# Strassen's form of the last FFN's output product, and a filter product in quarters of the array

## The chip, the core and the metric

The kernel runs on one core of a Trainium2 chip. The metric is the device time of one execution in microseconds, as the median of several executions. The engines are called PE (TensorE; PEld is its weight load), DVE (VectorE), ACT (ScalarE), POOL (GpSimd) and SP (SyncE); SP, ACT and POOL also issue DMAs.

## What is computed

The reference has two blocks, in fp32. The first is a long convolution with a filter that a small MLP makes; the second is a maxout FFN over all tokens of its result.

```python
# x, v: (4, 12544, 128); pos_emb: (12544, 64); w1: (64, 64); w2: (64, 128)
h_filt = (np.maximum(pos_emb @ w1, 0.0) @ w2) * np.exp(-0.01 * pos)[:, None]
u = x * v
y = irfft(rfft(u, n=2 * S, axis=1) * rfft(h_filt, n=2 * S, axis=0), n=2 * S, axis=1)[:, :S]
z = (x * y).reshape(4 * 12544, 128)
# moe_w1, moe_w2, moe_w3: (128, 768); moe_w_out: (768, 128)
out = np.maximum(np.maximum(z @ moe_w1, z @ moe_w2), z @ moe_w3) @ moe_w_out
```

## The kernel before

**The Fourier transform** has length 128 x 90 and is done in two steps by matrix products: a first one with `f1`/`f1h` (`first_halves`, L141), twiddle products with a table `wt` in 45 pieces `g` (`g_second`, `g_third`, both through `halves_mm`, L132), and a last one with `f4`/`f4p` (`t_last`). `halves_mm` puts a 128-column weight as two matmuls of 64 columns into the two column halves of the array. Each fp32 matmul shows as two instructions (two passes) in the trace.

**The order of work** is written out by hand; each engine runs its instructions in that order.
- *Start.* 30 warm-up products on zeros, then eight pairs of `mlp_in` (PE, L303: quarters on the diagonal, posT as the weight) and `mlp_out` (DVE, L311: relu and window). `window_back`, two small PE steps that turn the window around, stands behind the first `mlp_in`. Then the first transform of the filter's hidden units and of batch 0's `u`, with the conversion of the FFN weights on DVE beside it.
- *Filter and batch 0.* A loop over `s` of 45 pieces and three to drain. In each, PE runs `g_third(0, s-3)`, `s_second(s)` (L674: the filter's second transform step, real and imaginary parts in the two column halves), `g_second(s)` and `s_filter(s-1)` (L688: the product with w2, here `w2x`, which holds w2 twice, once with a minus sign on the real half, so that both parities of the spectrum come out of one product with K = 128 and 256 columns). ACT copies out `zs` (L444, then it issues its DMA), `G` (L678), `eo` (L163), makes `xs` (L413, L414) and copies `ht` (L693). DVE runs the butterfly (L157, L158), then `g_re` (L419), `g_im` (L423, L424) and `g_unfold` (L431); POOL issues the two DMAs of `ht` to `hd` (L695).
- *FFN.* 128 tiles of 392 tokens (32 per batch). The maximum of three is taken as one part plus the maximum of 0 and two differences: `w_sb[1]` and `w_sb[2]` hold differences to `w_sb[0]`, and `lin` = w1 times w_out is the linear part. For each of six blocks `f` of 128 hidden units, `up` runs two products (pa, pb), ACT takes relu of pa (L545), DVE the maximum with pb (L548); one step later `down` adds the product with `wo_sb[:, f]` to `ops`. Behind the last block ACT copies `ot` (L561) and issues its DMA. `t_load` (SP) fetches a tile's `zt` and `xT`; `t_last` makes its input `g` two steps ahead of use. Beside the FFN of batches 0 to 2 the next batch's convolution runs (`conv_steps`); beside that of batch 3, nothing. There POOL is idle.

Of the kernel before, what the change touches and what calls it, by code (L numbers as in the profile page):

```python
# [9 lines left out]
FP32 = mybir.dt.float32  # L10
# [5 lines left out]
P = 128  # L16
# [54 lines left out]
def kernel(  # L71
# [42 lines left out]

    w_sb = [const.tile([D, DFF], FP32, name=f"w_sb{i}") for i in range(3)]
    wo_sb = const.tile([P, NF, D], FP32, name="wo_sb")
    lin = const.tile([D, D], FP32, name="lin")
    eye = const.tile([P, P], FP32, name="eye")
    f1 = const.tile([NB, 2 * N1], FP32, name="f1")
# [105 lines left out]
    pro = ExitStack()  # L225
    pin = pro.enter_context(tc.tile_pool(name="pin", bufs=1))
    lwp = pro.enter_context(tc.tile_pool(name="lwp", bufs=3))
    fin = ExitStack()
# [13 lines left out]
    w2_in = sml.tile([P, D], FP32, name="w2_in")  # L242
    w2x = pin.tile([P, 2, D], FP32, name="w2x")
    win = sml.tile([64 + HH, P], FP32, name="win")
# [44 lines left out]

    def signs():  # L290

        for sg, lo_, m in ((0, 0, 1.0), (0, FO, 1.0), (1, 0, -1.0), (1, FO, 1.0)):
            nc.scalar.mul(w2x[lo_:lo_ + FO, sg].rearrange("f (c g) -> f c g", c=GC),
                          w2_in[lo_:lo_ + FO].rearrange("f (g c) -> f c g", c=GC), m)


# [216 lines left out]
    def t_last(i):  # L513
        zt = zts.pop(i)
        ps = cps.tile([P, 512], FP32, tag="cv", name="yps")
        g = hp.tile([D, 4, NB], FP32, tag="g", name="gt", bufs=2)
        y = ps[:, 0:N].rearrange("d (p n) -> d p n", p=4)
# [21 lines left out]

    def up(i, f):  # L540
        rhs = gs[i][:].rearrange("d p n -> d (p n)")
        h = hp.tile([P, N], FP32, tag="hid", name="hid")
        pa = hps.tile([P, 512], FP32, tag="hps", name="pa")
        halves_mm(pa[:, 0:N], w_sb[1][:, f * P:(f + 1) * P], rhs, True, True)
        nc.scalar.activation(h[:], pa[:, 0:N], Relu)  # L545
        pb = hps.tile([P, 512], FP32, tag="hps", name="pb")
        halves_mm(pb[:, 0:N], w_sb[2][:, f * P:(f + 1) * P], rhs, True, True)
        nc.vector.tensor_tensor(out=h[:], in0=h[:], in1=pb[:, 0:N], op=ALU.max)  # L548
        return h

    def down(i, f, h):
        if f == 0:
            pos_[i] = ops.tile([D, 512], FP32, tag="ops", name="ops")
            halves_mm(pos_[i][:, 0:N], lin[:], gs[i][:].rearrange("d p n -> d (p n)"), True,
                      False)
        halves_mm(pos_[i][:, 0:N], wo_sb[:, f, :], h[:], False, f == NF - 1)
        if f < NF - 1:
            return
        gs.pop(i)
        o = op_.tile([D, 4, NB], FP32, tag="o", name="ot")  # L560
        nc.scalar.copy(o[:].rearrange("d p n -> d (p n)"), pos_.pop(i)[:, 0:N])  # L561
        dst = outT.rearrange("d (p b n) -> d p b n", b=B, n=NB)[:, 4 * i[1]:4 * i[1] + 4, i[0], :]
        nc.scalar.dma_start(dst, o[:])

    def run(steps):
# [34 lines left out]

    warm_up(30)
    raws.append(load_raw(*jobs[0], nc.sync))
# [5 lines left out]
    for i in range(9):  # L608
        if i < 8:
            mlp_in(i)  # L610
        if i == 0:
            window_back()
        if i:
            mlp_out(i - 1)
    signs()
    mps.close()
# [42 lines left out]
    pl = sps.tile([D, 512], FP32, name="pl")  # L659
    Gs = {}  # L660

    def fold(f):
# [4 lines left out]
        return lambda: halves_mm(pl[:, 0:D], w1t[:, 0], wo_sb[:, f, :], f == 0, f == NF - 1)  # L667

    def s_second(g):

        ps = gps.tile([P, 512], FP32, tag="g", name="gps")
        for k in range(2):
            for r in range(2):
                nc.tensor.matmul(ps[64 * r:64 * r + 64, k * P:(k + 1) * P],  # L674
                                 specH[:, 2 * g + k, r, :], wf[g][:, k, r, :],
                                 start=(k == 0), stop=True, skip_group_check=True)
        G = cvp.tile([P, 2, 2, 64], FP32, tag="G", name="G", bufs=2)
# [3 lines left out]
    def s_filter(g):  # L681

        G = Gs.pop(g)
        ps = sps.tile([P, 1024], FP32, tag="h", name="sps")
        for c in range(2):
            for k in range(2):
                for h in range(2):
                    nc.tensor.matmul(  # L688
                        ps[64 * h:64 * h + 64, (2 * c + k) * 2 * D:(2 * c + k + 1) * 2 * D],
                        G[:, k, c], w2x[:].rearrange("p s d -> p (s d)"), start=(k == 0),  # L690
                        stop=True, skip_group_check=True)
        ht = cvp.tile([P, 2, 2, 2, D], FP32, tag="ht", name="ht", bufs=2)
        nc.scalar.copy(ht[:].rearrange("p c k q d -> p (c k q d)"), ps[:])  # L693
        for c in range(2):
# [6 lines left out]
    muls = dict(zip((NK - 13, NK - 11, NK - 10, NK - 5, NK - 3, NK - 1), range(EARLY)))  # L701
    turns = {NK - 9: 0, NK - 4: 2}
    for s in range(NK + 3):
        if s >= 3:
# [4 lines left out]
        if s < NK:  # L709
            ws[s, 0] = wf[s]  # L710
            s_second(s)
            g_second(s)
            wf.pop(s)
# [35 lines left out]

    hp = ctx.enter_context(tc.tile_pool(name="hp", bufs=3))  # L750
    f4p = hp.tile([N1, 2, NB // 2], FP32, name="f4p", bufs=1)
    nc.scalar.dma_start(f4p[:], f4p_d)
    inq = ctx.enter_context(tc.tile_pool(name="inq", bufs=2))
    planes = [hp.tile([P, 2, 4, P], U16, name=f"planes{i}", bufs=1) for i in range(3)]
    for t in planes:
        nc.gpsimd.memset(t[:].rearrange("p h s n -> p (h s n)"), 0)
    op_ = ctx.enter_context(tc.tile_pool(name="op", bufs=2))
    wp = ctx.enter_context(tc.tile_pool(name="wp", bufs=3))
    hh = ctx.enter_context(tc.tile_pool(name="hh", bufs=3))
    cvp = ctx.enter_context(tc.tile_pool(name="cvp", bufs=3))  # L760
    cps = ctx.enter_context(tc.tile_pool(name="cps", bufs=4, space=PSUM))
    hps = ctx.enter_context(tc.tile_pool(name="hps", bufs=3, space=PSUM))
    ops = ctx.enter_context(tc.tile_pool(name="ops", bufs=1, space=PSUM))
    state = {"turn": cps, "pair": (wp, hh), "cv": (cvp, cps), "xb": 3}


    tiles = [(b, i) for b in range(B) for i in range(NT)]
    late = None
    for n, (b, i) in enumerate(tiles):
        if i == 0:  # L770
            beside = {}
            if b + 1 < B:
                beside = conv_steps(b + 1, EARLY if b == 0 else 0)
        if n == 0:
# [3 lines left out]
        for f in range(NF):  # L778
# [9 lines left out]
            late = ((b, i), f, h)  # L788
            if f == 3 and n + 1 < len(tiles):
                t_last(tiles[n + 1])  # L790
            s = i * NF + f
            run(beside.pop(s, ()))
            if s == NT * NF - 1:
                assert not beside, sorted(beside)
    down(*late)


# [35 lines left out]
```

## Time and profile before

| | us |
|---|---|
| median of 4 runs | 2415.91 (2413.43 to 2422.55) |
| the profiled execution | 2414.46 |
| its span in the profile | 2412.3 |
| PE busy | 2394.4 |
| DVE busy | 1286.0 |
| ACT busy | 1026.5 |
| POOL busy | 314.3 |

The span runs from the first to the last instruction of the program; the profiled execution's own time has 2.2 us more around it. In lines of the timeline the columns are the start, the duration, the engine, the source line and the operation with its output and inputs, the number of instructions merged, and in brackets the engine's idle time before it with what ended it. Matmuls are pipelined, so their durations overlap, and the distance of starts is their pace. In a table by stretches the columns are the stretch, its length, busy time and instructions of PE, PEld, DVE, ACT and POOL, the granted TensorE clock, the DMA share and GB/s. Lines of the chain hold start, duration and work.

### The profile page before, as it was taken

Reading aid. Unit: us, or ns where it says so; the run is one execution under the profiler, and the core shown is the slowest. Engines: PE = TensorE matmul, PEld = TensorE weight load, DVE = VectorE, ACT = ScalarE, POOL = GpSimd, SP = SyncE. Lnnn points to the kernel's source line nnn. Section 1 sums busy time; section 2 is a strip of 40 time slices with the busy share of each in tenths; the row PEclk is TensorE's granted clock in tenths of the full one; section 3 lists DMA queues with packets and bytes.
Section 4 is the critical chain, followed back from the end, with each engine's and each line's share of the span. In section 5 each row is a group of like instructions: output and inputs, shape, how many; then the busy total and the mean of one; then the engine's idle time right before and its main releaser. Section 6 shows DMA issues by size and latency. Waiting matters only on the chain.

```text
span 2412.3 us, 63290 instructions
## 1 busy us (share of the span) xinstructions
PE 2394.4 (99%) x26089; PEld 1464.8 (61%) x26089; DVE 1286.0 (53%) x2719; ACT 1026.5 (43%) x1981; POOL 314.3 (13%) x349
## 2 busy tenths in 40 slices
PE   8999999999999999999999999999999999999999
PEld 7988866665555646666656546666665654444444
DVE  4678844456666635446666644546666642222222
ACT  2688843344444434444444424444444432222222
POOL 1022211011111111101111111101111100000000
PEclk9999999999999999999999999999999999999999
DMA  6878979777777659967787859978777842222221
GB/s 147 202 219 268 291 162 185 162 190 195 210 195 214 179 116 191 180 172 212 207 218 203 228 125 179 192 157 219 210 216 211 211 116 62 54 63 53 64 53 36
DMA packets 544553, 408.21 MB, mean 169 GB/s; under 512 B 390244, under 2 KB 436381, under 8 KB 544265
## 3 DMA queue, kind: packets, MB, share of 16 engines
q1 hardware_dynamic: 421760, 315.25, 54.7%
q10 hardware_dynamic: 117129, 74.31, 10.7%
q0 software_dynamic: 5376, 14.62, 2.2%
q8 instruction: 205, 3.36, 0.6%
q14 instruction: 83, 0.68, 0.1%
HBM read 295.76 MB, written 84.67 MB: 158 GB/s over the span
## 4 chain that ended last, share of the span: by engine, by line
PE 97%; DMA 1%; ACT 0%; DVE 0%; issue 0%; ACTq 0%; POOL 0%; SPq 0%; DVEq 0%
PE ops L132 24%; PE pb L132 21%; PE pa L132 21%; PE ps L132 13%; PE ps L141 8%; PE yps L132 5%; PE sps L688 3%; PE pm L303 1%; PE pst L341 1%; PE gps L674 1%; DMA specH<-in_pos_emb_dram 0%; DMA zd<-zs 0%; DMA hd<-ht 0%; DMA ut<-in_xr_dram 0%; ACT ht L693 0%
## 5 line engine op out<-in xcount | busy, mean ns | idle before, releaser
L548 DVE TENSOR_TENSOR hid<-hid,pb 128x392 f32<-128x392 f32 x768 | 431.8, 562 | 789.2 <-PE pb L132 506.1
L545 ACT ACTIVATE hid<-pa 128x392 f32<-128x392 f32 x768 | 381.9, 498 | 797.8 <-PE pa L132 628.4
L132 PE MATMUL pa<-gt,w_sb 128*64 128x392 f32 x3072 | 640.6, 493 | 0.7 <-DVE gt L533 0.7
L132 PE MATMUL pb<-gt,w_sb 128*64 128x392 f32 x3072 | 639.6, 492 | 1.4 <-ACT hid L545 1.2
L132 PE MATMUL ops<-hid,wo_sb 128*64 128x392 f32 x3072 | 639.5, 492 | 0.1
L132 PEld LDWEIGHTS pb<-gt,w_sb 128*64 128x64 f32 x3072 | 225.7, 137 | 283.1 <-issue 256.4
L132 PEld LDWEIGHTS ops<-hid,wo_sb 128*64 128x64 f32 x3072 | 226.8, 137 | 279.2 <-issue 228.4
L424 POOL TENSOR_TENSOR xt<-xt,xs 128x512 f32<-128x512 f32 x135 | 172.3, 1277 | 969.0 <-DVE xs L423 774.0
L132 PEld LDWEIGHTS pa<-gt,w_sb 128*64 128x64 f32 x3072 | 201.7, 137 | 110.9 <-issue 67.5
L141 PEld LDWEIGHTS ps<-f,uT 98*64 98x64 f32 x4096 | 178.1, 137 | 47.5 <-issue 44.8
L132 PEld LDWEIGHTS ps<-ab,wt 128*64 128x64 f32 x2880 | 168.6, 137 | 51.2 <-issue 26.6
L132 PE MATMUL ps<-ab,wt 128*64 128x128 f32 x2880 | 190.8, 274 | 1.0 <-DVE ab L431 0.9
L132 PEld LDWEIGHTS ps<-spec,wt 128*64 128x64 f32 x2880 | 168.0, 137 | 37.9 <-issue 34.2
L132 PE MATMUL ps<-spec,wt 128*64 128x128 f32 x2880 | 189.4, 273 | 1.4 <-issue 1.4
L141 PE MATMUL ps<-f,uT 98*64 98x90 f32 x4096 | 188.3, 241 | 0.0
L449 DVE TENSOR_TENSOR zs<-ps,z 128x256 f32<-128x256 f32 x270 | 102.0, 419 | 96.7 <-ACT z L447 94.5
L413 ACT ACTIVATE xs<-xt 64x512 f32<-64x512 f32 x180 | 113.2, 629 | 72.2 <-DVE xt L158 59.8
L431 DVE TENSOR_TENSOR ab<-xt 128x256 f32<-128x256 f32 x360 | 136.0, 419 | 1.6
L356 POOL COPY planes<-ut 128x784 uint16<-128x784 uint16 x90 | 76.5, 850 | 426.7 <-DVE ut L336 306.9
L419 DVE TENSOR_TENSOR xt<-xt,ht 128x512 f32<-128x512 f32 x180 | 124.2, 690 | 14.3 <-ACT ht L693 13.9
L145 ACT COPY spec<-ps 128x360 f32<-128x360 f32 (+1 forms) x132 | 71.7, 546 | 136.1 <-PE ps L141 136.0
L132 PEld LDWEIGHTS yps<-f4p,zt 90*64 90x64 f32 x3072 | 107.2, 138 | 34.5 <-issue 33.1
(86 smaller groups left out, 1827.7 us busy)
## 6 DMA issues: line engine op xcount, KB each, us to landing
wt<-wt_const SPq DMA_DIRECT2D x360, 256.0 KB, 4.8
ht<-hd SPq DMA_DIRECT2D x270, 256.0 KB, 4.7
zd<-zs ACTq DMA_DIRECT2D x180, 256.0 KB, 4.7
zt<-zd SPq DMA_DIRECT2D x192, 180.0 KB, 4.0
ut<-in_xr_dram SPq DMA_DIRECT2D x128, 196.0 KB, 3.7
ut<-in_vr_dram SPq DMA_DIRECT2D x128, 196.0 KB, 4.3
xT<-in_x_dram SPq DMA_DIRECT2D x512, 49.0 KB, 3.2
out_dram<-ot ACTq DMA_DIRECT2D x128, 196.0 KB, 4.0
```

Of the source, the lines that this page charges most:

```text
L132: nc.tensor.matmul(out[64 * h:64 * h + 64], lhsT[:, 64 * h:64 * h + 64], rhs, start=start, stop=stop, skip_group_check=True)
L141: nc.tensor.matmul(ps[64 * c:64 * c + 64, 256 * i + r * N1:256 * i + (r + 1) * N1], a[:, r, :], table[:, c * N1:(c + 1) * N1], start=(i % ...
L145: copy(dst, ps[:].rearrange("p (s m) -> p s m", m=256)[:, :, 0:2 * N1].rearrange("p s (r k) -> p k r s", r=2))
L356: nc.gpsimd.tensor_copy(pl_[:, :, :, 0:NB], a[:].bitcast(U16).rearrange("p s (n h) -> p h s n", h=2))
L413: nc.scalar.mul(xs[0:64], xt[64:128], -1.0)
L419: nc.vector.tensor_tensor(out=xt[:], in0=xt[:], in1=hts[g][:, 0], op=ALU.mult)
L424: (nc.gpsimd if apart else nc.vector).tensor_tensor(out=xt[:], in0=xt[:], in1=xs[:], op=ALU.add)
L431: nc.vector.tensor_tensor(out=ab[:, :, q, :], in0=y[:, :, 0, :], in1=y[:, :, 1, :], op=op)
L449: nc.vector.tensor_tensor(out=zs[:, a], in0=ps[:, 0:256], in1=z1[:], op=op)
L545: nc.scalar.activation(h[:], pa[:, 0:N], Relu)
L548: nc.vector.tensor_tensor(out=h[:], in0=h[:], in1=pb[:, 0:N], op=ALU.max)
L688: nc.tensor.matmul(ps[64 * h:64 * h + 64, (2 * c + k) * 2 * D:(2 * c + k + 1) * 2 * D], G[:, k, c], w2x[:].rearrange("p s d -> p (s d)"), ...
```

## The change

**The last FFN.** The 32 tiles of batch 3 are taken in pairs (`X`, `Y`: two PSUM banks). With the two tiles' hidden units split into blocks 0 to 2 and 3 to 5, and w_out split in rows (the same) and columns (64 each), the product is a 2 x 2 block product. It is done with seven block products instead of eight (Strassen's form in Winograd's order of sums): sums S1 to S4 of the hidden tiles on POOL (12 operations of 128x392 a pair, `sum_`), differences of w_out's blocks once on DVE (`tw`, and `b12` in place), and sums of the products by ACT copies (`copied`) and DVE adds from PSUM (`added`). In each block product the two halves of the token columns go to the two column halves of the array with the same 64-column weight (`mm`): 196 columns each. The linear part is split in the same way and added to four of the seven. A pair has 12 steps, each with one `up`; the products of a pair follow 9 steps later (`LAG`), 25 groups spread over 12 steps, and those of the last pair run on behind its last `up`. The outputs leave through eight DMAs a pair, issued by POOL. `gt` gets four buffers in place of two. The pools of the convolution are closed ahead of the stage, and their SBUF and PSUM space is used anew.

**The filter.** `s_second` computes both signs: for q = 0 and 1 it writes into column half q the sum over r of specH times `wf`, with the real part's weight negated for q = 1. POOL makes that negated copy a step ahead (`s_minus`). `s_filter` then multiplies, for each q, 64 rows of `G` with plain w2 (64 rows, in either half of the partitions): 16 matmuls of K = 64, 64 columns and 128 moving columns in the four quarters of the array, in place of 8 with K = 128 and 256. `signs` (four ACT operations) becomes `w2_order` (one).

**The start.** `window_back` moves from behind the first `mlp_in` to behind 22 warm-up products, with 3 more behind it (30 before). `eye` and `w_sb[0]` move to a pool that ends earlier.

```diff
+    def s_minus(g):
+        m = cvp.tile([P, 2, FO], FP32, tag="minus", name="minus", bufs=1)
+        nc.gpsimd.tensor_single_scalar(m[:], specH[:, 2 * g:2 * g + 2, 0], -1.0, op=ALU.mult)
+        minus[g] = m
     def s_second(g):
         for k in range(2):
             for r in range(2):
-                nc.tensor.matmul(ps[64 * r:64 * r + 64, k * P:(k + 1) * P],
-                                 specH[:, 2 * g + k, r, :], wf[g][:, k, r, :],
-                                 start=(k == 0), stop=True, skip_group_check=True)
+                for q in range(2):
+                    lhsT = m[:, k] if q and r == 0 else specH[:, 2 * g + k, r, :]
+                    nc.tensor.matmul(ps[64 * q:64 * q + 64, k * P:(k + 1) * P],
+                                     lhsT, wf[g][:, k, r, :],
+                                     start=(k == 0 and r == 0), stop=True,
+                                     skip_group_check=True)
     def s_filter(g):
-        for c in range(2):
+        for ri in range(2):
             for k in range(2):
-                for h in range(2):
-                    nc.tensor.matmul(
-                        ps[64 * h:64 * h + 64, (2 * c + k) * 2 * D:(2 * c + k + 1) * 2 * D],
-                        G[:, k, c], w2x[:].rearrange("p s d -> p (s d)"), start=(k == 0),
-                        stop=True, skip_group_check=True)
+                for q in range(2):
+                    for h in range(2):
+                        at = 512 * q + (2 * ri + k) * D
+                        nc.tensor.matmul(
+                            ps[64 * h:64 * h + 64, at:at + D],
+                            G[64 * q:64 * q + 64, k, ri, :], w2x[64 * q:64 * q + 64],
+                            start=(ri == 0 and k == 0), stop=True, skip_group_check=True)
...
+    ORDER = (("h11", 0), ("h21", 0), ("h11", 1), ("h22", 0), ("h21", 1), ("h11", 2),
+             ("h21", 2), ("h22", 1), ("h22", 2), ("h12", 0), ("h12", 1), ("h12", 2))
+    SUMS = {2: (s3, 0), 4: (s2, 0), 5: (s3, 1), 7: (s3, 2), 8: (s2, 1), 9: (s2, 2),
+            10: (s1, 0), 11: (s1, 1), 12: (s1, 2), 13: (s4, 0), 14: (s4, 1), 15: (s4, 2)}
+        def mm(ps, w, rhs, start):
+            for c in range(2):
+                nc.tensor.matmul(ps[64 * c:64 * c + 64, 0:H2], w, rhs[:, H2 * c:H2 * c + H2],
+                                 start=start, stop=True, skip_group_check=True)
+        plan = (
+            (X, "h11", wo_sb[:, 0:NC, 0:64], True, None, [(copied, "p1", X)], None),
+            (Y, "s2", tw[:, 0], True, None, [(added, "u2", "p1", Y)], None),
+            (X, "h12", wo_sb[:, NC:, 0:64], False, (m1, first), [(copied, "c11", X)], None),
+            (Y, "s3", tw[:, 1], False, (m2, second_), [(added, "u3", "p1", Y)], None),
+            (X, "h21", wo_sb[:, 0:NC, 64:128], True, None, [(added, "c22", "u3", X)], None),
+            (Y, "h22", tw[:, 2], True, (linx[:], second_), [(added, "c21", "u3", Y)],
+             (stored, 0)),
+            (X, "h12", wo_sb[:, NC:, 64:128], False, (m2, first), [(added, "c12", "u2", X)],
+             (stored, 1)),
+        )
...
+            if j in (5, 8) and i + 2 < NT:
+                t_last((b, i + 2 + (j > 5)))
-    warm_up(30)
+    warm_up(22)
+    window_back()
+    warm_up(3)
```

## The prediction

> **What bounds the kernel now.** I read the page first (the chain that ended last), then the chain by time, then the timeline of the two places that the change touches.
>
> ```profile
> PE 97%; DMA 1%; ACT 0%; DVE 0%; issue 0%; ACTq 0%; POOL 0%; SPq 0%; DVEq 0%
> ```
>
> TensorE (PE) carries 97% of the chain, so a change is worth the PE time that it takes out, where PE stays the bound. First the last FFN, in the timeline of PE around 2108 us:
>
> ```profile
> 2107.49 1.09 PE L132 MATMUL yps<-f4p,zt 90*64 90x49 f32 x32
> 2108.41 0.84 PE L132 MATMUL pa<-gt,w_sb 128*64 128x392 f32 x4
> 2109.08 0.83 PE L132 MATMUL pb<-gt,w_sb 128*64 128x392 f32 x4
> 2109.74 0.83 PE L132 MATMUL ops<-hid,wo_sb 128*64 128x392 f32 x4
> ...
> 2121.85 0.84 PE L132 MATMUL pa<-gt,w_sb 128*64 128x392 f32 x4
> ```
>
> Starts count, not durations (ends overlap): a product with 392 columns takes 0.658 us (two column halves side by side, two passes), yps 0.92, a tile 13.44 = 19 x 0.658 + 0.92. There is no gap: here PE alone sets the time. Now the loop that makes the filter's spectrum and batch 0 (45 iterations), in the timeline around 204 us:
>
> ```profile
> 202.29 0.37 ACT L678 COPY G<-gps 128x256 f32<-128x256 f32 x1 [0.44 <-ACT zs L444]
> 202.35 1.90 PE L688 MATMUL sps<-w2x,G 128*64 128x256 f32 x16
> 203.60 0.62 ACT L414 COPY xs<-xt 64x512 f32<-64x512 f32 x1
> 204.08 1.06 PE L132 MATMUL ps<-ab,wt 128*64 128x128 f32 x16
> 204.29 1.01 ACT L693 COPY ht<-sps 128x1024 f32<-128x1024 f32 x1
> 204.97 0.61 PE L674 MATMUL gps<-wt,specH 128*64 128x128 f32 x8
> 205.34 0.69 DVE L419 TENSOR_TENSOR xt<-xt,ht 128x512 f32<-128x512 f32 x1 [0.27 <-ACT ht L693]
> 205.41 1.04 PE L132 MATMUL ps<-spec,wt 128*64 128x128 f32 x16
> 206.23 0.37 ACT L678 COPY G<-gps 128x256 f32<-128x256 f32 x1 [0.44 <-ACT zs L444]
> 206.28 1.90 PE L688 MATMUL sps<-w2x,G 128*64 128x256 f32 x16
> ```
>
> PE is full: 1.73 + 0.89 + 0.44 + 0.87 = 3.93 us. But ScalarE (ACT) goes from G to G in 3.94 us, and its only slack is from the end of xs (204.22) to ht (204.29): its own floor is 3.87. The 0.44 before G is its own DMA issue. VectorE (DVE) idles 0.27 of 3.95: its floor is 3.68. Three engines lie within 7% of each other.
>
> **1. Strassen's product, PE.** A pair of tiles loses 2 x 7 products (6 w_out, 1 linear) at 0.658 = 9.21 us, and gets 7 x 3 + 4 = 25 groups of 196 columns. The trace has no 196. Per pass of both halves, 128 columns take 0.109 (0.87 for 8), 256 take 0.216 (1.73 for 8), 392 take 0.329; the line through the first two gives 0.166 at 196, so 0.332 a group and 8.30 a pair. That is -0.91 a pair and **-14.6 us** for 16. Bounds: exactly half of 0.658 gives -15.8; the pace of L141's 90-column groups (0.86 ns a column) gives -12.4.
>
> **2. What hides the rest of it.** Twelve POOL sums a pair: the nearest row is L424, 1.277 us for 128x512, so 0.98 by columns; eight output DMAs from POOL at the 0.53 us of hd<-ht. Together 16.0 us beside 25.97 us of PE a pair (12 steps of 2.16). ACT loses half of its output copies, and DVE gets five adds of 128x196 (below the 0.42 of a 128x256) against more than half its time idle. The tightest wait is on s2(2). From the start of step 7 POOL runs: the first four stores (the c21 add waits in DVE's queue behind gt, which waits for the linx product that frees its buffer: ready at about 2.0) to 4.1, s3(2) 5.1, s2(1) 6.1, four stores 8.2, s2(2) 9.2. PE asks at 4 x 2.16 + 1.32 = 9.96: 0.76 to spare. If that cover goes, each 0.1 us that a sum is dearer costs 0.3 us a pair. Behind gt in DVE's queue stands one hid maximum, whose pb bank PE wants two steps later: no stall.
>
> **3. The ends.** In the last step the first half of the products is not hidden by later work. Before, the last up ends at 2406.53 and the span at 2412.3:
>
> ```profile
> 2406.53 1.79 PE L132 MATMUL ops<-hid,wo_sb 128*64 128x392 f32 x8
> 2408.36 0.49 ACT L561 COPY ot<-ops 128x392 f32<-128x392 f32 x1 [1.78 <-PE ops L132]
> ```
>
> That is 5.77 us, of which 1.32 is product work. After the last up now come 20 groups = 6.64 us, the drain and the c12 add to 7.2; but POOL is still issuing c21's stores (6.1 to 8.2), then c12's, the last issued from 9.8, and landing as long after its issue as before (2408.88 to 2412.3, 3.4): 13.2. Tail: (13.2 - 6.64) - (5.77 - 1.32) = **+2.1**. Where the stage begins, the first pa takes a PSUM bank that the last ot copy (0.49 and its latencies) must leave: **+0.75**.
>
> **4. The filter loop.** gps doubles (0.44 to 0.87). The w2 product becomes 16 products of 128 columns in quarters. If four run at once, 8 x 0.109 = 0.87, and not under 0.92, the quickest that the trace issues 32 such instructions (yps). The only row in row halves is L303: two DVE operations per 64 instructions every 2.32 us, 36 ns each, so 1.16; its weights are strided, so I take 1.0. If row halves do not overlap, 16 x 0.109 = 1.75. On top comes the change of tile form: in the chain, 8 full-array transposes between column halves take
>
> ```profile
> 77.17 1.01 PE pst L341 x8
> 78.18 2.63 PE ps L141 x64
> 80.81 1.01 PE pst L341 x8
> ```
>
> 3.64 a round, where 8 x 0.109 and 64 instructions at the undisturbed pace (2.48, two of ACT's 1.24 us rounds) make 3.35: 0.14 a switch, 0.28 an iteration. The Trainium skill says the same against this change (TensorEngine Tiling (Array Packing), Key Properties): changing the tiling mode, not just the tile, drains the array. If the rule did not hold between these forms, the PE sum below would be 0.28 less, and ACT's floor would decide.
> PE: 3 x 0.88 + 1.0 + 0.28 = 3.92 (3.84 to 4.67). ACT: unchanged work, 3.87. DVE: the new sign operation (128x128 on POOL; 0.14 us by L356's pace to 0.32 by L424's) may block it:
>
> ```profile
> L419 DVE TENSOR_TENSOR xt<-xt,ht x180: 681/685/1353, 129.9 to 1951.0; 128x512 f32<-128x512 f32 x180
> L424 POOL TENSOR_TENSOR xt<-xt,xs x135: 1264/1277/1289, 491.8 to 1953.0; 128x512 f32<-128x512 f32 x135
> ```
>
> The one L419 of 1353 ns began while an L424 ran. The new operation waits for s_second, which ends while DVE is in its five two-input operations, so I charge it in full: 3.68 + 0.14 to 0.32 = 3.82 to 4.00. The skill has the rule (SBUF — State Buffer, on the shared port pair): a VectorE operation with two SBUF inputs and a GpSimd operation that reads SBUF exclude each other for a whole instruction. By the rule DVE pays; if POOL always gave way, the iteration would be 3.92 or 3.87 by PE or ACT.
> All three land near today's 3.93: **0 us**. The best case is ACT's floor, -0.06 x 45 = -2.7; L303's pace gives PE 4.08, +6.8.
>
> **5. The start.** mlp_in(0) still begins at 20.40, when its DMAs land, but window_back no longer stands behind it (PE from 24.17 to 25.69). The granted clock:
>
> ```profile
> 26.00:28.00 2.00, 2.00 (x44) 2.00 (x42) 1.29 (x2) 1.68 (x5) 0.00 (x0) 0.50 1.13 277
> 30.00:32.00 2.00, 2.00 (x62) 2.00 (x60) 0.97 (x2) 0.00 (x0) 0.00 (x0) 1.00 0.34 73
> ```
>
> It is 0.50 until 28 and 1.00 from 30. Without the break it may rise sooner; a mlp_in takes 3.64 at the low clock, 2.32 at the full one. Worth 1.5 for the break and up to 1.5 for the clock; loads may take some back: **-1.5** (-3 to 0). w2_order instead of the signs, and the moved eye and w_sb0, cost nothing: ACT idles there until 46 us.
>
> **Sum:** -14.6 + 2.1 + 0.75 + 0 - 1.5 = -13.2. The profiled execution took 2414.46 (span 2412.3 and 2.2 around it); the median of the four runs is 1.45 higher: 2402.5 as a median.
>
> **The rivals.** *Quarters do not overlap (slower).* The w2 product then takes 1.75, PE 3 x 0.88 + 1.75 + 0.28 = 4.67, +0.74 x 45 = +33: 2436. For it: no row shows two row halves on the same columns. Against it: L303's two corners do start 10 ns apart. It eats the whole gain once the iteration passes 3.93 + 13.2/45 = 4.22, a product of 1.30. Chance 0.12.
> *The loop gets a little longer* (L303's pace, or DVE held for more than 0.3): 4.05 to 4.1, +5 to +8: 2407 to 2411. For it: three engines without slack. Chance 0.18.
> *POOL bounds the last FFN.* From 1.23 us a sum PE waits for s2(2); at 1.54 the pair's 0.91 is gone; at 1.78 POOL is full (12 x 1.78 + 4.5). At 1.8 each pair takes 1.7 us longer than forecast: 2430. Against it: L424 never left 1264 to 1289 with DVE at work beside it. Chance 0.04.
> *The forecast*, with its bounds 2396 to 2406: 0.66.
>
> **The numbers.** 2402.5. The range 2396 to 2413 holds the forecast and the longer loop (0.84). A difference of 0.3% (7 us) is what a measurement of this kernel can tell from none: under 2408.7 lie the forecast and half of the longer loop, 0.75; no change 0.09; slower 0.16.
>
> **What would show it.** In the changed profile: groups of 196 columns every 0.33 us without gaps ahead of them, a pair in 26.0, POOL sums of 1.0, hardly any wait of PE on POOL, the stage's first pa waiting for ot; G to G in 3.87 to 4.0; 32 quarter instructions in 0.9 to 1.2; L419 at times longer than 0.69; mlp_in without window_back's break. A loop over 4.2, PE waiting for s2, or 196 columns over 0.18 a pass would make the prediction wrong.

## The result, and the profile after

The changed kernel takes 2418.20 us (median of 36 runs), the kernel before 2414.63 (median of 59): the ratio is 1.0016, 95% interval [1.0011, 1.002]. It is 3.6 us slower, inside the 0.3% that the prediction called no change, where 13.2 less was forecast. The profiled execution has a span of 2415.3 us against 2412.3.

The page's chain by engine:

```profile
PE 90%; ACT 3%; issue 2%; DVE 2%; DMA 1%; POOL 1%; ACTq 0%; POOLq 0%; DVEq 0%
```

PE carried 97% of it before. Seven points went to ACT, DVE and "issue" (time in which an engine waited for nothing that the profile shows), where the forecast had put nothing. Three marks in both traces (starts, us) show where:

| stretch | before | after | difference |
|---|---|---|---|
| start of the span to the loop's first gps | 124.21 | 121.26 | -2.95 |
| first gps to the FFN's first pa | 197.71 | 209.36 | +11.65 |
| first pa to the gt of batch 3's first tile | 1652.27 | 1654.33 | +2.06 |
| from there to the end | 438.13 | 430.32 | -7.81 |

**The loop.** The timeline of one chain through two iterations, DVE, ACT and PE:

```profile
201.13 1.19 PE L131 MATMUL ps<-ab,wt 128*64 128x128 f32 x16
...
202.15 0.27 PE L775 MATMUL gps<-wt,specH 128*64 128x128 f32 x1
...
203.02 1.04 PE L131 MATMUL ps<-spec,wt 128*64 128x128 f32 x16
...
203.99 1.10 PE L793 MATMUL sps<-w2x,G 64*64 64x128 f32 x32
204.11 0.37 ACT L162 COPY eo<-ps 128x256 f32<-128x256 f32 x1
...
204.51 0.63 ACT L411 ACTIVATE xs<-xt 64x512 f32<-64x512 f32 x1
...
205.15 0.62 ACT L412 COPY xs<-xt 64x512 f32<-64x512 f32 x1
205.48 1.21 PE L131 MATMUL ps<-ab,wt 128*64 128x128 f32 x16 [0.38 <-DVE ab L429]
205.79 1.01 ACT L798 COPY ht<-sps 128x1024 f32<-128x1024 f32 x1
...
206.84 0.69 DVE L417 TENSOR_TENSOR xt<-xt,ht 128x512 f32<-128x512 f32 x1 [0.22 <-ACT ht L798]
...
208.89 0.76 DVE L429 TENSOR_TENSOR ab<-xt 128x256 f32<-128x256 f32 x2
209.40 0.33 PE L131 MATMUL ps<-ab,wt 128*64 128x128 f32 x2
```

The quarters run as forecast: PE's part is 1.02 (third, from 201.13 to the next gps at 202.15), 0.87 (gps), 0.97 (g_second) and 1.04 (the w2 product, taken from the undisturbed sequence of e1_swap below), in all 3.9 where 3.92 was reckoned. Yet PE waits for ab, and from G to G there are by turns 3.92 and 4.34 us, on the mean 4.13. The lines above close a ring, a chain of dependences that comes back to where it began: the third product starts at 201.13, g_second is far enough for eo at 204.11, two xs and ht follow on ACT until 206.80, DVE makes ab out of this ht, and ab starts the third product two iterations on, at 209.40. Once round is 8.27, two iterations: 2.98 + 0.40 + 1.28 + 1.01 + 2.60.

Before, the same ring was shorter. The third product that the prediction shows at 204.08 led to this line, 2.42 later:

```profile
206.50 0.38 ACT L163 COPY eo<-ps 128x256 f32<-128x256 f32 x1
```

With the same 5.29 behind it (1.28 + 0.40 on ACT, 1.01 and 2.60) that is 7.71, 3.86 an iteration, just under PE's 3.93. The doubled gps (+0.44) and a form switch added 0.56 to the ring; the w2 product that became 0.7 shorter does not lie on it.

**The end of the loop**, in the timeline:

```profile
321.33 0.33 PE L755 MATMUL pt<-eye,w_sb 128*128 128x128 f32 x1
...
321.77 2.73 POOL L866 MEMSET planes<- 128x1024 uint16 x3 [8.77 <-issue]
...
321.79 1.02 SPq L497 DMA_DIRECT2D zt<-zd  x1
...
327.02 2.79 PE L131 MATMUL yps<-f,zt 90*64 90x98 f32 x32 [2.04 <-DMA zt<-zd]
```

The planes' memset and the load of zt begin together, when the last transpose of w_sb[0] by eye is over: both tiles now lie in the pool whose space they take. PE waits 2.04 us for zt, and then works at a lower granted clock (the column behind POOL's busy time). In slices of 2 us it is 0.50 from 328 to 334 and 1.00 from there, so the 0.75 in the second line is a mean of the two:

```profile
328.00:332.00 4.00, 3.19 (x29) 2.06 (x27) 0.57 (x1) 0.00 (x0) 0.00 (x0) 0.50 0.66 145
332.00:336.00 4.00, 4.00 (x22) 1.62 (x20) 1.12 (x2) 1.00 (x2) 0.00 (x0) 0.75 1.08 223
```

**The last FFN.** Steady pairs are as forecast, in the groups (busy, mean ns) and in the distance of yps in the timeline:

```profile
L606 PE MATMUL ops<-hid,wo_sb 128*64 128x196 f32 x768 | 82.2, 329 | 0.0
L576 POOL TENSOR_TENSOR s<-hid,s 128x392 f32<-128x392 f32 x48 | 49.5, 1032 | 31.0 <-DVE hid L546 31.0
```

```profile
2103.56 1.09 PE L131 MATMUL yps<-f4p,zt 90*64 90x49 f32 x32
...
2129.52 1.09 PE L131 MATMUL yps<-f4p,zt 90*64 90x49 f32 x32
```

A pair takes 25.96 (26.89 before), a sum 1.03, a store on POOL 0.61. The losses are at three single places. At the beginning (timeline):

```profile
1994.88 0.89 ACT L543 ACTIVATE hid<-pa 128x392 f32<-128x392 f32 x2 [3.88 <-DMA out_dram<-ot]
...
1995.43 0.88 PE L131 MATMUL pa<-gt,w_sb 128*64 128x392 f32 x4 [1.53 <-ACT hid L543]
```

The new pool's hid waits until the last ot has landed in memory. In the third pair POOL is late for s2:

```profile
2058.95 0.59 POOL L630 DMA_DIRECT2D out_dram<-o  x1 [2.79 <-issue]
...
2065.00 0.55 PE L606 MATMUL ops<-s,tw 128*64 128x196 f32 x4 [0.57 <-POOL s L576]
```

And in the last pair, where it then issues the eight last stores in a row:

```profile
2401.87 0.55 PE L606 MATMUL ops<-s,tw 128*64 128x196 f32 x4 [1.02 <-POOL s L576]
...
2407.59 4.77 POOL L630 DMA_DIRECT2D out_dram<-o  x8
```

POOL's closing drain (the DRAIN instructions at the end of its program; min/median/max ns, first and last start) comes last: the longest of the three runs to 2414.49, and the span ends at 2415.27:

```profile
L989 POOLq DRAIN  x3: 46/93/3744, 2410.7 to 2415.0; - x3
```

In a steady pair s2(2) is in time by 2.1 us (POOL and PE in the timeline; the sum ends at 2114.87):

```profile
2113.82 1.05 POOL L576 TENSOR_TENSOR s<-hid,s 128x392 f32<-128x392 f32 x1
...
2116.97 0.50 PE L606 MATMUL ops<-s,tw 128*64 128x196 f32 x4
```

### The profile page after: what moved, and what is told of

It is laid out like the page before. It is cut to its first block, busy times and chain, and to the rows that moved or that the text cites. A ratio compares the mean times of both kernels' runs of the same rounds, so it can differ in the third digit from the quotient of the medians.

```text
span 2415.3 us, 67441 instructions
## 1 busy us (share of the span) xinstructions
PE 2381.4 (99%) x27853; PEld 1513.9 (63%) x27853; DVE 1311.1 (54%) x2804; ACT 1021.0 (42%) x1978; POOL 626.9 (26%) x714
## 4 chain that ended last, share of the span: by engine, by line
PE 90%; ACT 3%; issue 2%; DVE 2%; DMA 1%; POOL 1%; ACTq 0%; POOLq 0%; DVEq 0%
PE pb L131 21%; PE pa L131 21%; PE ops L131 18%; PE ps L131 10%; PE ps L140 7%; PE yps L131 6%; PE ops L606 5%; ACT ht L798 1%; ACT xs L411 1%; PE pm L301 1%; PE pst L339 1%; DVE xt L422 1%; DVE xt L417 1%; PE pw L131 1%; DVE xs L421 1%
## 5 line engine op out<-in xcount | busy, mean ns | idle before, releaser
L131 PE MATMUL ops<-hid,wo_sb 128*64 128x392 f32 x2304 | 479.1, 492 | 0.0
L422 POOL TENSOR_TENSOR xt<-xt,xs 128x512 f32<-128x512 f32 x135 | 172.5, 1278 | 968.0 <-DVE xs L421 770.6
L131 PEld LDWEIGHTS ops<-hid,wo_sb 128*64 128x64 f32 x2304 | 169.2, 137 | 209.5 <-issue 168.2
L429 DVE TENSOR_TENSOR ab<-xt 128x256 f32<-128x256 f32 x360 | 136.0, 419 | 1.6
L417 DVE TENSOR_TENSOR xt<-xt,ht 128x512 f32<-128x512 f32 x180 | 124.2, 690 | 21.2 <-ACT ht L798 21.2
L421 DVE TENSOR_TENSOR xs<-xs,ht 128x512 f32<-128x512 f32 x180 | 123.3, 685 | 0.0
```

The source lines that it names most:

```text
L131: nc.tensor.matmul(out[64 * h:64 * h + 64], lhsT[:, 64 * h:64 * h + 64], rhs, start=start, stop=stop, skip_group_check=True)
L417: nc.vector.tensor_tensor(out=xt[:], in0=xt[:], in1=hts[g][:, 0], op=ALU.mult)
L421: nc.vector.tensor_tensor(out=xs[:], in0=xs[:], in1=hts.pop(g)[:, 1], op=ALU.mult)
L422: (nc.gpsimd if apart else nc.vector).tensor_tensor(out=xt[:], in0=xt[:], in1=xs[:], op=ALU.add)
L429: nc.vector.tensor_tensor(out=ab[:, :, q, :], in0=y[:, :, 0, :], in1=y[:, :, 1, :], op=op)
```

## The experiments

Runs of the kernel before, made beside each group of experiments, are the base: 2414.41, 2413.39, 2414.13, 2415.65 and 2414.11 us. "Ratio" is to that base, with its 95% interval.

**1. The ring: e1_swap.** The edit, on the changed kernel:

```diff
-            s_second(s)
+            g_second(s)
+            s_second(s)          # without its copy G
...
-            g_second(s)
...
             s_filter(s - 1)
+        if s < NK:
+            s_copy(s)            # the copy G, now behind ht
```

> The changed kernel, with two steps of the filter loop reordered: on PE g_second(s) comes ahead of s_second(s), and ACT's copy G(s) stands behind the copy ht(s-1). The same instructions, in the same number. Theory A (a cycle over two iterations: ab on DVE, third on PE 1.04, the doubled gps 0.87 on PE, g_second, eo 0.40, xs 0.64, xs 0.64, ht 1.01 on ACT, 2.58 on DVE to the next ab, in all 8.27 = 2 x 4.13): gps and G leave the cycle, the floor of ACT or PE decides, so from G to G 3.87 to 3.95 instead of 4.13, and the kernel 8 to 11 us under the changed one: 2407 to 2410 (ratio to the kernel before 0.997 to 0.998). Theory B (PE with its form switches, or the sign operation on POOL holding up DVE, sets the iteration): the work is the same, so 4.13 from G to G stays, and 2418.

2404.53 us, ratio 0.9959 [0.9946, 0.9971]. From G to G there are 3.895 us nearly throughout. PE in the timeline:

```profile
206.33 1.18 PE L131 MATMUL ps<-ab,wt 128*64 128x128 f32 x16
207.34 1.04 PE L131 MATMUL ps<-spec,wt 128*64 128x128 f32 x16
...
209.18 1.10 PE L797 MATMUL sps<-w2x,G 64*64 64x128 f32 x32
210.22 0.44 PE L131 MATMUL ps<-ab,wt 128*64 128x128 f32 x4
```

PE is now full: third 1.01, g_second and gps 1.84, the w2 product 1.04. The same instructions in another order are 13.7 us quicker than the changed kernel, more than the 8 to 11 expected. In the trace the first gps to the first pa take 196.05 instead of 209.36: 7.9 of the 13.3 lie between the first and the last G (some iterations at the end still take 4 to 5 us), the rest at the loop's two ends; 1.2 of it because the first yps ran at the full clock here although it waited 1.70 us for zt (2.39 us from yps to pa, 3.60 in the changed kernel).

**2. Half of the reordering: e9_pe_order.**

```diff
-            s_second(s)
-            if s + 1 < NK:
-                s_minus(s + 1)
-            g_second(s)
+            g_second(s)
+            s_second(s)
+            if s + 1 < NK:
+                s_minus(s + 1)
```

> The changed kernel with half of e1_swap's reordering: PE runs g_second(s) ahead of s_second(s), but ACT's copy G(s) stays ahead of xs, now right behind eo. Theory A (the cycle): from third, G now waits on ACT for g_second and gps behind it (1.04 + 0.97 + 0.87 + 0.2), then 0.37 for G, and xs begins at 3.45 instead of 3.40: the cycle keeps its length, 4.13 to 4.2 from G to G, 2418 to 2421. Theory B (e1_swap gained because the even-odd step comes earlier on PE as such): 3.9, and 2405 to 2409.

2414.85, ratio 1.0004 [0.9996, 1.0013]. From G to G 3.89 and 4.36 by turns, 8.25 for two: the ring has kept its length. The median is some 3 us under what theory A gave; the profiled run, with a span of 2415.1, is as long as that of the changed kernel (2415.3), though its stretch from the first gps to the first pa is 2.8 shorter, all of it outside the first to the last G. The pace decides between the theories: with G, and so gps, still ahead of xs on ACT, PE's order alone does not help.

**3. The order in the kernel before: e12_order_before.** The edit of e1_swap, on the kernel before.

> The kernel before, with the order of e1_swap in its filter loop. Theory A: there PE is full (3.93) and gps is only 0.44 of the cycle, so the order brings nothing: 3.93 from G to G, 2413 to 2415. Theory B: the order is a gain of its own and has nothing to do with the doubled gps: 5 to 10 us less, 2404 to 2409.

2414.85, ratio 1.0002 [0.9993, 1.0011]; 3.91 and 3.96 from G to G. The order is no gain of its own; it only undoes what the doubled gps did.

**4. The sign operation: e8_one_sign.**

```diff
-            if s + 1 < NK:
-                s_minus(s + 1)
...
-        m = minus.pop(g)
+        m = minus[0]
```

> The changed kernel, with the sign operation done once ahead of the filter loop, and its result (that of piece 0) used by all pieces: 44 of the 45 sign operations on POOL are left out, all else stays. Theory A (the cycle through the doubled gps sets the iteration): 4.13 from G to G stays, 2418. Theory B (the sign operation, 1.01 us in the loop, holds up DVE through the port that they share, as my prediction charged it): 3.95 to 4.0 from G to G, 6 to 8 less, 2410 to 2412.

2417.44, ratio 1.0015 [1.0006, 1.0024], where the changed kernel has 1.0016; 4.13 from G to G. The sign operation costs nothing in this loop.

**5. The parts alone, on the kernel before.** The filter's part, e3_filter:

```diff
+            if s + 1 < NK:
+                s_minus(s + 1)
...                              # with s_second, s_filter, w2x and w2_order of the change
```

> The kernel before, with the filter's part of the change alone (both signs in s_second, the sign operation on POOL, the w2 product in quarters, w2_order). Theory A: from G to G 4.13 on the mean (two iterations 8.27) and the first G 1.2 later: +8.7, 2423. Theory B (the part as I forecast it, and the loss in the changed kernel comes from its other parts, such as the place of eye and w_sb[0]): 3.92 and 2413 to 2415.

2422.87, ratio 1.0035 [1.0023, 1.0048]: +8.5. From G to G 4.13. The place of two tiles, e2_pin:

```diff
-    eye = const.tile([P, P], FP32, name="eye")
...                              # w_sb[0] leaves const as well
+    eye = pin.tile([P, P], FP32, name="eye")
+    w_sb[0] = pin.tile([D, DFF], FP32, name="w_sb0")
```

> The kernel before, with nothing changed but the place of eye and w_sb[0]: from the pool that stays to the pool that closes ahead of the FFN. Theory A: the first zt and the planes take over that pool's space and wait for the last transpose of w_sb[0] on PE; the first yps then waits for the DMA of zt, PE idles, its granted clock falls, and the first FFN starts 1.5 to 3 us later and runs its first microseconds at a low clock, up to 2 more: 2 to 5 us in all, 2417 to 2420. Theory B: the late start of the first FFN comes from the longer loop (DMA landings) alone: 0, so 2414.6.

2417.37, ratio 1.0013 [1.0004, 1.0022]: +3.0, and the wait is there with the old loop (timeline; the second line is the same place in the kernel before):

```profile
317.96 1.57 PE L131 MATMUL yps<-f,zt 90*64 90x98 f32 x32 [1.52 <-DMA zt<-zd]
```

```profile
319.63 1.57 PE L132 MATMUL yps<-f,zt 90*64 90x98 f32 x32 [0.68 <-DVE spec L145]
```

So the load adds 0.84 to a wait that PE had already. The granted clock falls to 0.55 and 0.60 behind it (slices of 4 us), and from this yps to that of the next tile there are 14.25 us instead of 10.24. The lower clock is not tied to the wait for zt, though: from the first FFN yps to the second, six of the ten traces without the moved tiles have 10.2 to 10.3 and four have 12.0 to 12.2 (e5_strassen, e10_all, e12_order_before, e14_all_no_pool_stores), all behind the old wait of 0.68; of the eight with them e1_swap has 10.34 and seven have 12.0 to 14.3. That the longer wait makes the drop more frequent and longer is likely from these counts, but not shown. The start, e4_start:

```diff
-    warm_up(30)
+    warm_up(22)
+    window_back()
+    warm_up(3)
...
-        if i == 0:
-            window_back()
```

> The kernel before, with window_back alone moved behind 22 warm-up products and 3 behind it. Theory A: the loop's first gps 2.9 earlier (121.3 instead of 124.2), of which all stays: 2411.7. Theory B: what is gained at the start is lost to loads that are not there yet, or comes from the new place of w_sb[0]: 0 to -1, 2413.6 to 2414.6.

2413.17, ratio 0.9993 [0.9984, 1.0001]: -1.2, and the interval reaches 1. The loop's first gps comes at 122.31 instead of 124.21, but over all traces it lies between 120.3 and 124.5 with the moved window_back (twelve, mean 122.35) and between 121.7 and 124.2 without (six, mean 122.86): most of the 2.95 between the two traces of above is scatter. The trace that the prediction worked from is a late one: its mlp_in begins at 20.40, in the other five without the move at 18.5 to 19.5. The last FFN, e5_strassen:

```diff
-        g = hp.tile([D, 4, NB], FP32, tag="g", name="gt", bufs=4)
+        own = i[0] == B - 1 and i[1] % 4 > 1
+        g = (lp if own else hp).tile([D, 4, NB], FP32, tag="g2" if own else "g", name="gt", bufs=2)
...                              # eye and w_sb[0] in const; filter and start as before
```

> The kernel before, with the last FFN's part of the change alone: eye and w_sb[0] stay where they were, and gt has two buffers in hp and two in lp, so that the memory suffices. Theory A (the part brings less than forecast: the steady pair is 25.96 as reckoned, but hid waits for ot's DMA at the stage's beginning, 1.7, POOL is late once for s2 in the third pair, 0.8, and once in the last, 1.0): 7 to 8 under the kernel before, 2406.5 to 2407.5. Theory B (the part brings the forecast 11.75, and the rest was lost elsewhere): 2402.7.

2405.73, ratio 0.997 [0.996, 0.9979]: -7.7. The four parts add up to 8.5 + 3.0 - 1.2 - 7.7 = +2.6, against +3.6 for the whole.

**6. The stage's beginning: e6_ot_stays.**

```diff
-    op_ = conv.enter_context(tc.tile_pool(name="op", bufs=2))
+    op_ = ctx.enter_context(tc.tile_pool(name="op", bufs=2))   # ahead of conv's pools
```

> The changed kernel, with the pool of ot kept open, so that the pool lp of the last FFN does not take over its space. Theory A: the first hid no longer waits for ot's DMA, the gap of 2.02 between starts on PE at 1993 goes: 1.7 less, 2416.5. Theory B: the wait for ot's DMA only stands ahead of the differences of w_out on DVE or another wait, which then come last: 0, 2418.2.

2414.99, ratio 1.0005 [0.9996, 1.0013], where the changed kernel has 1.0016. From the first pa of the stage to that of the second pair there are 20.04 us instead of 21.95: theory A. What comes last now is DVE's work on w_out, without harm:

```profile
1992.56 0.50 ACT L543 ACTIVATE hid<-pa 128x392 f32<-128x392 f32 x1 [1.03 <-DVE linx L924]
```

**7. The tail.** e7_stores moves the last FFN's output DMAs from POOL:

```diff
-                    nc.gpsimd.dma_start(
+                    (nc.sync if i + 2 < NT else (nc.sync, nc.scalar, nc.gpsimd, nc.sync)[2 * n + c]).dma_start(
```

> The changed kernel, with the last FFN's output DMAs issued by SP instead of POOL, and those of the last pair by SP, ACT and POOL in turn. Theory A: POOL has 4.8 us less work a pair, is not late for s2 any more (0.8 in the third pair, 1.0 in the last), and the last stores, which POOL issued one after the other for 4.8 us, are out some 3 us sooner: 4 to 5 less, 2413 to 2414. Theory B: stores in SP's queue wait for their sums and hold the loads of zt and xT behind them; gt comes late and PE waits: 2418 or more.

2420.71, ratio 1.0031 [1.0019, 1.0042]: a miss for theory A, but not by theory B either. POOL is never late for s2, all pairs take 25.96, PE does not wait for loads. The tail grew: from the last pb to the end 18.3 us instead of 14.9, although SP saw the last store landed at 2407.2. What ended last was POOL's closing drain, 10.6 us long. e10_all, below, had 15.2 at that place, with its drain 2.7 us behind SP. So two runs with no store from POOL at all (in the first, SP issues all but half of the last pair's, which ACT does):

```diff
-                    nc.gpsimd.dma_start(
+                    (nc.scalar if i + 2 >= NT and c else nc.sync).dma_start(
```

> The changed kernel, with the last FFN's output DMAs issued by SP, those of the last pair by SP and ACT in turn, and none by POOL. Theory A (POOL's closing drain waits long for DMAs that POOL issued shortly before): without such DMAs the drain is short as in the kernel before; POOL is not late for s2 (0.8 in the third pair, 1.0 in the last); from the last pb to the end 11 to 12 us instead of 14.9, and the kernel 4 to 5 under the changed one: 2413 to 2414. Theory B (the stores themselves, or POOL's sums, set the end): as e7_stores, 18 us from the last pb to the end, 2417 to 2421.

2418.59, ratio 1.0009 [1.0, 1.0018]; 14.65 from the last pb to the end. Both theories missed: the late end does not need stores that POOL issued. The last sums in the timeline, and the closing drains (min/median/max ns, first and last start):

```profile
2403.61 2.97 POOL L576 TENSOR_TENSOR hid<-hid,s 128x392 f32<-128x392 f32 x3 [2.26 <-DVE hid L546]
```

```profile
L989 POOLq DRAIN  x3: 46/98/11927, 2404.3 to 2416.7; - x3
L989 SPq DRAIN  x3: 7/7/13, 2413.1 to 2416.5; - x3
```

The long drain runs from 2404.30 to 2416.23, 9.65 us beyond the end of the last sum (2406.58), while SP was through at 2413.1. The same in the repaired kernel:

> As e10_all, with the last FFN's output DMAs issued by SP, those of the last pair by SP and ACT, none by POOL. Theory A (the drain): from the last pb to the end 11 to 12 us instead of 15.2, 2396 to 2397. Theory B: 2400 as e10_all, or more.

2402.39, ratio 0.9949 [0.9935, 0.9963]; 14.64 from the last pb to the end, and the drain ends 9.64 behind the last sum. To see whether a sum is enough, e16_one_pool_op adds one to the kernel before:

```diff
+            if n == len(tiles) - 1 and f == 4:
+                probe = hp.tile([P, N], FP32, tag="turned", name="turned", bufs=3)
+                nc.gpsimd.tensor_tensor(out=probe[:], in0=h[:], in1=h[:], op=ALU.add)
```

> The kernel before, with one operation more: a sum of 128x392 on POOL of the last tile's hid of block 4 with itself, into a buffer that nobody reads. It runs from about 2405.4 to 2406.4, beside PE, and nobody waits for it. Theory A: POOL's closing drain ends 9.6 us after it, at 2416.1, instead of 2411.6: the span grows by 4 to 5 us, 2418 to 2419. Theory B (the late drains of the other runs belong to their stores or to the length of POOL's work): 0, as the kernel before.

2418.22, ratio 1.0018 [1.0009, 1.0026]: one operation of 0.84 us that nobody waits for costs 4.1 us.

```profile
2403.69 0.84 POOL L791 TENSOR_TENSOR turned<-hid 128x392 f32<-128x392 f32 x1 [451.23 <-DVE hid L548]
```

```profile
L831 POOLq DRAIN  x3: 46/98/10519, 2403.7 to 2414.7; - x3
L831 SPq DRAIN  x3: 7/7/13, 2409.6 to 2414.4; - x3
```

2403.66 + 10.52 = 2414.18, 9.65 behind the sum, and SP was through at 2409.6. So the other way, e15_last_sums_dve:

```diff
-        nc.gpsimd.tensor_tensor(out=out[:], in0=a[:], in1=b[:], op=op)
+        (nc.vector if state.get("last") else nc.gpsimd).tensor_tensor(out=out[:], in0=a[:], in1=b[:], op=op)
```

> As e14_all_no_pool_stores, with the twelve sums of the last pair on DVE instead of POOL. Theory A (POOL's closing drain ends some 9.6 us after its last sum, whatever it issued): POOL's last sum lies over 20 us before the end, the drain is long over, and the end follows SP's sight of the last store by 0.75 as in the kernel before: from the last pb to the end 11.5 instead of 14.6, and 3 us under e14_all_no_pool_stores, 2399. Theory B: the end stays, or DVE is now late for the tail's adds: 2402 or more.

2395.96, ratio 0.9931 [0.9917, 0.9944]; 11.46 from the last pb to the end, 3.2 less than e14_all_no_pool_stores, as theory A has it. The median is 6.4 less; in the traces another 1.7 of it is the first FFN, which had the lower clock in e14_all_no_pool_stores and not here. The long drain is now over before the end, and SP's sight of the last store decides:

```profile
L998 POOLq DRAIN  x3: 46/93/11334, 2361.6 to 2393.6; - x3
L998 SPq DRAIN  x3: 7/7/13, 2393.1 to 2393.4; - x3
```

**8. All repairs, and what the filter's part is worth.** e10_all is the changed kernel with the edits of e1_swap, e5_strassen's places of tiles, e6_ot_stays, and half as many stores, by taking token quarters 0 and 2 in one column half and 1 and 3 in the other:

```diff
-                nc.tensor.matmul(ps[64 * c:64 * c + 64, 0:H2], w, rhs[:, H2 * c:H2 * c + H2],
+                nc.tensor.matmul(ps[64 * c:64 * c + 64, 0:H2].rearrange("p (q n) -> p q n", q=2), w,
+                                 rhs.rearrange("p (q c n) -> p c q n", c=2, n=NB)[:, c],
```

> The changed kernel with four repairs: the order of e1_swap; eye and w_sb[0] in the pool that stays (gt in two and two buffers, as in e5_strassen); the pool of ot kept open; and the token halves of the last FFN's products taken alternately (quarter tiles 0 and 2, 1 and 3 of a tile), so that a pair's output leaves in four DMAs from POOL instead of eight. Theory A (the terms add up): e1_swap's 2404.5, less 3.0 (e2_pin), less 1.9 (the gap in e6_ot_stays), less 0.8 and 1.0 (POOL late for s2), less 2.4 (four issues of 0.6 at the end): 2395.4, between 2394 and 2398. Theory B (what is repaired at one place is lost at the next, since DMA landings or the granted clock set the start of the first FFN): 2400 to 2404.

2399.94, ratio 0.9941 [0.9927, 0.9955]. Less than the sum of the terms, for two reasons in its trace, which is of the slowest of the six runs (2404.67): the tail did not shrink (15.2, the drain), and its first FFN lost 1.7 us at a lower clock (0.68 from 320 to 324), though zt was there in time. e11_all_old_filter takes the filter of the kernel before instead, with that kernel's order.

> As e10_all, but with the filter of the kernel before (w2 product with K = 128, no sign operation, its order in the loop). Theory A: PE is the bound of both loops, 3.93 here and 3.89 there, so 1 to 2 us above e10_all, 2396 to 2398. Theory B: the quarters gain more than their PE time through ACT or DVE, 4 us or more above e10_all; or nothing at all, the same time as e10_all.

2400.81, ratio 0.9947 [0.9935, 0.996], 3.92 and 3.95 from G to G. The filter's part, once its order is mended, is worth about 1 us, which these intervals cannot tell from nothing. The fastest version, e15_last_sums_dve, is 18 us under the kernel before.

## Why the prediction was wrong

| step | forecast | measured | from |
|---|---|---|---|
| 1. Strassen's PE time | -14.6 | -14.9 | 16 x (26.89 - 25.96) |
| 2. POOL's cover | 0 | +0.8 | one pair of 26.76 |
| 3. the stage's beginning | +0.75 | +2.4 | waits of 0.75 and 1.69 |
| 3. the tail | +2.1 | +3.5 | last up to the end, less product work: 14.58 - 6.64, before 5.79 - 1.32 |
| 4. the loop | 0 | +8.5 | e3_filter |
| 5. the start | -1.5 | -1.2 | e4_start, interval reaching 0 |
| 5. the place of eye and w_sb[0] | 0 | +3.0 | e2_pin |

**Step 4 failed, and it decided the sign.** Its PE sum was right (3.9 for 3.92; the quarters overlap, 1.04 for 1.0; beside a switch of form g_second takes 0.97 instead of 0.87 and the third product 1.02 instead of 0.89, 0.10 and 0.13 for the forecast's 0.14), so "quarters do not overlap" is refuted. What was wrong is the conclusion "All three land near today's 3.93": it took the largest of three sums of busy time, as if the engines only had to be full. They pass work round a ring, and a ring has a length of its own. Its terms all stood in the trace of before: 7.71 for two iterations, 0.15 under what PE needed. Adding 0.56 made it 8.27, 4.13 an iteration; no engine is full at that pace. e1_swap, e9_pe_order and e12_order_before show it together. The rival "the loop gets a little longer" named the right place and too small a size (4.05 to 4.1), by other mechanisms. (The terms of the sum give 2402.7 as a median, not 2402.5; nothing hangs on it.)

**The charge on DVE was wrong.** The sign operation takes 0.53 us alone and in 36 of 45 pieces 1.01 beside DVE's work (timeline):

```profile
204.27 0.69 DVE L422 TENSOR_TENSOR xt<-xt,xs 128x512 f32<-128x512 f32 x1
204.33 1.01 POOL L763 TENSOR_SCALAR minus<-specH 128x128 f32<-128x128 f32 x1
```

It starts just behind L422, which keeps its 0.69, and the next operation (L429) takes 0.426 beside it and 0.418 without: POOL is the one that is stretched. In two pieces it starts first; then it takes 0.54 and L422 0.76. e8_one_sign shows that taking it away changes nothing here. The Trainium skill's rule (SBUF — State Buffer, on the shared port pair) gives the pair to the operation that starts first, for the whole instruction. The trace agrees in who is stretched at L422; "By the rule DVE pays" held in two pieces of 45, for 0.07 us each. L429, also with two SBUF inputs, ran beside the sign operation at nearly its own pace, which the rule does not have; spans on POOL are rough, though.

**Step 5, "the moved eye and w_sb0 cost nothing"**, looked at who uses them where they went, and not at who uses the space afterwards: zt and the planes, whose load stands at the head of the FFN. e2_pin shows +3.0: the wait for zt, 1.5 to 2.1 us where PE waited 0.7 before, and the lower clock that followed it in seven of eight traces. The price varies: where PE idled about as long, the clock fell to 0.5 in some runs and stayed at 1.00 in e1_swap.

**Steps 1 to 3.** The arithmetic of the pair held to 0.02 us. The margin for s2(2) is 2.1 in the steady pairs, not the 0.76 of step 2, which has four stores ahead of s3(2) where the trace has two. It went in the third pair and the last, behind gaps of 2.79 and 2.42 us ahead of a store on POOL. The first gap stands ahead of the 129th DMA that POOL issues in the program in all eight traces in which POOL issues that many, whatever the time; in those with fewer there is none. Why it is there no run shows. In step 3 the wait for ot's copy was 0.75 as forecast, but the wait of the new pool for ot's DMA was not seen: 1.7 (e6_ot_stays). The tail was 1.4 us longer than reckoned, 1.2 of it PE's wait for s2. POOL's drain decided there by a little: it ended at 2414.5 and SP was through at 2414.1. The span ends 0.78 behind that drain, as in e13_no_pool_stores and e16_one_pool_op; where SP decides, as in e15_last_sums_dve, it ends 0.84 behind SP. With quicker stores, as in e7_stores, the drain alone decides; the prediction reckoned with the stores and not with the drain.

## What to carry to other kernels

In a loop where engines hand on work, add up the longest ring of dependences over the iterations that it spans, beside each engine's busy time: once the ring is the longest of them, an operation that grows on it costs its full growth, one that shrinks off it gives nothing, and order may take an operation off it for free. When tiles move to a pool that ends sooner, list who takes over the space and what those must wait for, DMAs still under way included. Work that is moved to an idle engine can put off the end of the kernel even if nobody waits for its result.

## What was not expected of the hardware

- POOL's closing drain ended 9.65, 9.64 and 9.65 us behind its last sum in e13_no_pool_stores, e14_all_no_pool_stores and e16_one_pool_op. The kernel before has it too, out of sight: a drain of 10.95 that began at 1953.0 with POOL's last sum and ended 9.65 behind it. Where POOL issues stores behind the last sum it ended 13.3 behind it with two (e7_stores), 10.0 with four (e10_all) and 6.85 with eight (the changed kernel); why the stores change it is open.
- After 2.04 us of idling the granted clock stood at 0.50 for some 6 us in the changed kernel, and from the first yps to the second there were 13.20 us instead of 10.24. The same clock was seen in four traces behind an idle time of only 0.68 us, and not in e1_swap behind 1.70.
- POOL idled 2.3 to 2.8 us ahead of its 129th DMA, with nothing in the profile to wait for, in every trace in which it issued that many.
- The sign operation of 128x128 on POOL: 0.53 us alone, 1.01 beside DVE. The products beside a switch between column halves and quarters of the array took 0.10 and 0.13 us longer, which agrees with the drain that the Trainium skill states (TensorEngine Tiling (Array Packing), Key Properties) and gives it a price.
